# Eight more tiles of the first LayerNorm transposed by DMA, and a new order of all tasks, in a transformer block on one core

## The chip, the cores and the metric

One core of a Trainium2 chip runs the whole kernel. The metric is the device time of one execution in microseconds (us). Five engines work side by side, each through its own list of instructions in order: TensorE (PE; PEld is its loading of weights), VectorE (DVE), ScalarE (ACT), GpSimd (POOL) and SyncE (SP), which here only issues DMAs. The kernel before took 204.36 us, the median of 3 runs (204.16 to 204.45).

## What is computed

The block is an adaptive LayerNorm around linear attention, and a second one around a gated feed-forward layer, for 2048 tokens (S) of 512 channels (D), with 32 heads of 16 and F = 1376:

```python
mod = (silu(c) @ w_mod).reshape(6, 512)          # sa, ca, ga, sb, cb, gb
h = layernorm(x) * (1 + ca) + sa
q, k, v = split(h @ wqkv)                        # 32 heads of 16
pq, pk = q @ w_phi, k @ w_phi                    # per head
phi = lambda p: concat(softmax(p), softmax(-p))
kv, z = sum_s phi(pk) v, sum_s phi(pk)           # over all 2048 tokens
o = (phi(pq) @ kv) / (phi(pq) @ z + 1e-6)
x = x + ga * (o @ wo)
h = layernorm(x) * (1 + cb) + sb
x = x + gb * ((sigmoid(h @ w_gate) * (h @ w_up)) @ w_down)
```

## The kernel before

Tokens are cut into 16 tiles of 128. The kernel is written as a graph of about 1200 small tasks (`G.add`: a name, the engines that can run it, a function, what it reads and writes). The string `ORDER` (lines 40 to 101) lists every task once; `Graph.arrange` goes through it, takes for each task the engine behind an `@` or the first one of its choices, and gives buffers out; `emit` issues the instructions in that order. Each engine then runs its own tasks in the order of the list and waits where an input or a buffer isn't ready. So one string sets the order on all engines, and SP's too.

The stages, by the names of their tasks:

- Loads (`ld_...`, all on SP): x in seven pieces (`x0a` to `x3a`), wk, wv, parts of w_mod (`wm00a` to `wm01b` for sa and ca, `wmga` for ga, `wmm2` for the rest), wo, and the feed-forward weights. All of SP's DMAs go through one queue (q1 of the page).
- `warm`: matmuls on zeros at the start; their results aren't used.
- `modc1.0`, `modc1.1` (line 630): the two halves of sa and ca on TensorE, from the w_mod loads.
- `fold` (line 679): w_phi is multiplied into wq and wk, so that one matmul gives pq or pk. A fold needs the transposed weights `wT_sb`. For the keys (side 1) TensorE transposes them (`tpw`), for the queries (side 0) a DMA does, straight from wqkv in DRAM (`wqT0` to `wqT3`, line 669). `foldc` copies the result on ACT.
- First LayerNorm, for groups of one or two tiles (`LG`): `st1` and `rs1` (statistics), `nmr1`, `xn1` (normalized tile), then the transposition into `h1T`, and `hm1` (times 1+ca plus sa, four tasks a group). The list `TD` says how a group is transposed: 0 by TensorE (`tph`, line 744, into PSUM, from which `hm1` reads on ACT or DVE), 1 by a DMA transpose from SP (`xT1`, line 736, straight into `h1T`, and `hm1` works in place on ACT, POOL or DVE). Before, only groups 6 and 7 (tiles 10 to 13) have a 1.
- Keys and values: for each tile `K` (line 817), `e` (two exponentials on ACT), `n` (sums, DVE line 780), `r` (reciprocal), `phi` (product, POOL or DVE), `V` (line 821), `va`, and `kv` (line 282), which adds into two PSUM banks over all tiles. K of tiles 0 to 7 and V of tiles 0 to 3 are two halves (`K0a`, `K0b`), each with two of the four blocks of channels.
- `kvn`, `kvz`: the sums are masked and go to SBUF. Nothing of the attention's output can start before.
- Queries: `Q` (line 871), `qe`, `qn`, `qphi`, and `pT`, a DMA transpose. Some of them run among the keys, the others later.
- Output, by tile: `num` (line 326), `rd`, `u`, the transposition `oT` (by TensorE for tiles 0 and 1 as `tpo`, else by DMA), `out` (line 356, with wo times ga, made by `wo0` to `wo3` on POOL), `x1_` (residual), `st2`, `rs2`, `nmr2`, `xn2`, `xnT`, `mod` (second LayerNorm).
- Feed-forward, in six chunks of 1, 1, 2, 4, 4 and 4 tiles: `g` and `u` (line 447), `tg` (tanh on ACT, after the table load `tsw`), `hm` (DVE), `y` (line 485), `fin`, `st` (store).

The `warm` tasks, `K`, `V`, `Q` and the folds all stand in TensorE's one list.

Of the kernel before, what the change touches and what calls it, by code (L numbers as in the profile page):

```python
# [43 lines left out]
wqT1 hm1_22 hm1_13@A hm1_03 xn1_7 K1a K0a hm1_02@A hm1_23@A xn1_6 tph42 tph40 xn1_5 hm1_40@A st1_8 tph41 ld_x3a xn1_4 K3a hm1_42 hm1_12@A ld_wv0 nmr1_6 tph43
K3b hm1_41@A xn1_11 tph30 xn1_10 st1_9 rs1_5@P hm1_30@A tph31 wqT3 tph32 K1b ld_wmga st1_15 st1_14 hm1_31@A fold01 foldc01 K0b tph33 wqT2 rs1_8@P K2a K2b
hm1_33 nmr1_5 V0a wqT0 V0b V3a xn1_9 e3.0 V1a xT1_11 e0.0 fold03 n3.0 V1b nmr1_8 xn1_14 va0 e2.0 n0.0 st1_13 r0.0 modca.0 modca.1 xn1_15 st1_12 xn1_8 foldc03
n2.0 modcac e1.0 hm1_32@A V2a fold02 phi0.0 n1.0 r1.0 fold00 V2b foldc02 foldc00 r3.0 va1 xT1_10 hm1_60@P ld_wmm2 va2 r2.0@A hm1_62@P tph82 hm1_82@A tph50
# [1011 lines left out]
```

## Time and profile before

| | |
|---|---|
| median of 3 runs | 204.36 us |
| profiled execution, span from first to last instruction | 202.6 us |
| TensorE busy | 195.7 us, 97% |
| DVE, ACT, POOL busy | 160.4, 106.1, 102.8 us |
| first key matmul | 13.84 us after the span's start |
| last group of `kv` matmuls starts | 56.10 us |
| first gate matmul (`g`) | 67.96 us |
| last `fin` starts | 199.23 us |
| granted TensorE clock | 1.000 |

The profile is of one execution. Its span is measured from the first to the last instruction; the runs' time holds some 1.8 us more. TensorE is called busy while a matmul is in its pipeline, so its share of 97% doesn't say how fast it goes; the distance between starts does. A row of the timeline gives start, length, engine, line, output and inputs, and the number of instructions merged, and in brackets how long the engine was idle before and what ended that.

### The profile page before, as it was taken

How to read it: one execution, taken by the hardware profiler on the slowest of the kernel's cores; microseconds unless marked ns; L12 is line 12 of the kernel's file. 1: busy time of each engine (PE TensorE's matmuls, PEld its weight loads, DVE VectorE, ACT ScalarE, POOL GpSimd, SP SyncE). 2: the span in 40 equal slices, each digit the busy share in tenths (PEclk: the TensorE clock that was granted, in tenths of full speed). 3: DMA queues.
4: the chain of work that ended last, by engine and by line, in shares of the span. 5: the costliest groups of instructions: out<-in, count | busy, mean ns of one | idle time of the engine just before them, and what ended most of it. 6: DMA issues, size and time to landing. Idle time of an engine off the chain costs nothing.

```text
span 202.6 us, 4159 instructions
## 1 busy us (share of the span) xinstructions
PE 195.7 (97%) x1471; PEld 106.2 (52%) x1471; DVE 160.4 (79%) x375; ACT 106.1 (52%) x252; POOL 102.8 (51%) x144
## 2 busy tenths in 40 slices
...
GB/s 173 329 248 265 264 237 119 111 80 290 402 204 71 137 102 59 80 28 108 128 75 84 53 71 84 102 107 53 26 26 81 2 78 52 31 3 22 33 53 55
DMA packets 49452, 22.92 MB, mean 113 GB/s; under 512 B 38065, under 2 KB 47634, under 8 KB 49426
## 3 DMA queue, kind: packets, MB, share of 16 engines
...
## 4 chain that ended last, share of the span: by engine, by line
PE 69%; DVE 14%; ACT 6%; issue 3%; POOL 3%; DMA 3%; SPq 1%; DVEq 0%; POOLq 0%
PE y_ps L485 19%; PE u_ps L447 18%; PE g_ps L447 17%; DVE ks L780 7%; PE a_ps L356 6%; DMA wqk_sb<-in_A_wqkv_dram 3%; PE num L326 2%; DVE kr L798 2%; ACT qe L776 2%; DVE phi L787 2%; PE q_ps L871 1%; PE g_ps L449 1%; ACT h1T L751 1%; DVE qks L780 1%; POOL phi L787 1%
## 5 line engine op out<-in xcount | busy, mean ns | idle before, releaser
L457 ACT ACTIVATE tg<-g_ps 128x512 bf16<-128x512 f32 (+5 forms) x66 | 28.8, 455 | 67.0 <-PE g_ps L447 39.4
L485 PE MATMUL y_ps<-wd_sb,wmod_sb 128*128 128x512 bf16 (+4 forms) x187 | 45.7, 367 | 0.0
L468 DVE SCALAR_TENSOR_TENSOR wmod_sb<-tg,u_ps 128x512 bf16<-128x512 bf16 (+4 forms) x63 | 30.2, 491 | 18.1 <-ACT tg L457 11.6
L447 PEld LDWEIGHTS <-wg_sb 128*128 128x128 bf16 (+1 forms) x252 | 21.9, 99 | 16.1
L447 PEld LDWEIGHTS <-wu_sb 128*128 128x128 bf16 (+1 forms) x252 | 21.9, 99 | 16.0 <-issue 0.3
L784 POOL TENSOR_TENSOR qphi<-qe,qks 128x512 bf16<-128x512 bf16 x24 | 25.1, 1062 | 4.4 <-DMA pT<-qphi 1.7
L485 PEld LDWEIGHTS <-wmod_sb 128*128 128x128 bf16 (+1 forms) x187 | 17.1, 98 | 16.0 <-issue 0.6
L447 PE MATMUL u_ps<-wT_sb,wu_sb 128*128 128x512 bf16 (+2 forms) x124 | 23.8, 322 | 0.0
L447 PE MATMUL g_ps<-wT_sb,wg_sb 128*128 128x512 bf16 (+2 forms) x124 | 23.2, 322 | 0.0
L447 PE MATMUL g_ps<-wqk_sb,wg_sb 128*128 128x128 bf16 (+4 forms) x128 | 20.0, 287 | 0.0
L447 PE MATMUL u_ps<-wqk_sb,wu_sb 128*128 128x128 bf16 (+4 forms) x128 | 19.8, 287 | 0.1
L780 DVE TENSOR_REDUCE qks<-qe 128x64 bf16<-128x1024 bf16 x16 | 19.2, 1206 | 0.0
L492 DVE TENSOR_TENSOR ot<-y_ps,x 128x512 bf16<-128x512 f32 (+2 forms) x17 | 11.1, 654 | 10.2 <-PE y_ps L485 10.1
L780 DVE TENSOR_REDUCE ks<-e 128x64 f32<-128x1024 bf16 (+2 forms) x22 | 19.1, 903 | 0.0
L376 POOL TENSOR_SCALAR ve<-mv 128x2 f32<-128x2 f32 (+1 forms) x8 | 1.8, 221 | 33.8 <-DVE mv L366 33.7
L776 ACT ACTIVATE e<-k_ps 128x512 bf16<-128x512 f32 (+2 forms) x44 | 18.2, 522 | 0.0
L776 ACT ACTIVATE qe<-q_ps 128x512 bf16<-128x512 f32 x32 | 17.4, 618 | 0.6 <-POOL phi L787 0.4
L817 PE MATMUL k_ps<-wqk_f,h1T 128*128 128x512 bf16 x64 | 16.5, 379 | 0.0
L356 PE MATMUL a_ps<-wo_sb,oT 128*128 128x512 bf16 x64 | 16.3, 379 | 0.0
L787 POOL TENSOR_TENSOR phi<-e,kr 128x1024 bf16<-128x1024 bf16 (+2 forms) x10 | 14.4, 1449 | 3.5 <-ACT kr L795 2.0
L821 PE MATMUL v_ps<-wv_sb,h1T 128*128 128x512 bf16 x64 | 16.1, 379 | 0.1
L871 PE MATMUL q_ps<-wqk_f,h1T 128*128 128x512 bf16 x64 | 15.9, 379 | 0.0
...
## 6 DMA issues: line engine op xcount, KB each, us to landing
...
```

The source lines that it names most:

```text
L356: pe.matmul(ap_[:], lhsT=oT[:, j, :], rhs=wo_sb[:, j, :], start=(j == 0), stop=(j == KT - 1))
L447: pe.matmul(ps[:fsz, 0:n], lhsT=w[:, j, ft * P:ft * P + fsz], rhs=h[:, j, 0:n], start=(j == 0), stop=(j == KT - 1))
L457: G.add(f"tg{k}.{ft}", {"ACT": 0.13 + n * 0.00083}, lambda e, tg=tg, g_ps=g_ps, fsz=fsz, n=n: act.activation(tg[:fsz, 0:n], g_ps[:fsz, 0:n ...
L468: dve.scalar_tensor_tensor(hm_all[:fsz, hm[k].slot, ft, 0:n], tg[:fsz, 0:n], 1.0, u_ps[:fsz, 0:n], op0=ALU.add, op1=ALU.mult)
L485: mm = pe.matmul(y[:, 0:c1 - c0], lhsT=hm_all[:fsz, hm[k].slot, ft, tl * P:(tl + 1) * P], rhs=wd_sb[:fsz, ft, c0:c1], start=(ft == 0), sto ...
L776: act.activation(ee[:, a:b, s].rearrange("p g f h -> p g (f h)"), kp[:, a * 64:b * 64].rearrange("p (g n) -> p g n", n=64), ACT.Exp, scale ...
L780: dve.tensor_reduce(ks[:, a:b].rearrange("p g s h -> p (g s) h"), ee[:, a:b].rearrange("p g s f h -> p (g s) h f"), axis=AX.X, op=ALU.add)
L784: engine(e).tensor_tensor(ph[:].rearrange("p (g s f h) -> p g s f h", s=2, f=DH, h=4)[:, :, s], ee[:, :, s], ks[:, :, 1 - s].unsqueeze(2). ...
L787: engine(e).tensor_tensor(ph[:, a * P:b * P].rearrange("p (g f h) -> p g f h", f=DH, h=4), ee[:, a:b].rearrange("p g s f h -> p (g s) f h" ...
L817: pe.matmul(kp[:], lhsT=h1T[:, j, t * P:(t + 1) * P], rhs=wqk_f[:, j, D:2 * D], start=(j == 0), stop=(j == KT - 1))
L821: pe.matmul(vp[:], lhsT=h1T[:, j, t * P:(t + 1) * P], rhs=wv_sb[:, j, :], start=(j == 0), stop=(j == KT - 1))
L871: pe.matmul(qp[:], lhsT=h1T[:, j, t * P:(t + 1) * P], rhs=wqk_f[:, j, 0:D], start=(j == 0), stop=(j == KT - 1))
```

## The change

Two things are changed. In `TD` groups 3, 4, 5 and 8, tiles 4 to 9, 14 and 15, get a 1: their 16 `tph` tasks, of two transposes each, are gone, and eight `xT1` tasks come in. `hm1` of these groups then reads and writes `h1T` in SBUF, so that POOL can run it too. And `ORDER` is another list, found by a search over the order and the engines of all tasks with a replay of measured times. The functions are the same; all lines below the list move up by one.

```diff
-TD = [0, 0, 0, 0, 0, 0, 1, 1, 0]
+TD = [0, 0, 0, 1, 1, 1, 1, 1, 1]
...
-wdz pmem warm0 ld_x0a st1_1 rs1_1 st1_0 c1 c2 ld_x0b warm1_0 warm1_1 warm1_2 warm1_3 ld_wk0 ld_wk1 nmr1_1 xn1_1@A st1_3 warm1_4 st1_2 rs1_0 xn1_0 tph11 tpw1
...
+wdz pmem bd warm0 ld_x0a st1_1 ld_x0b st1_2 rs1_1 st1_3 nmr1_1 st1_0 rs1_2 nmr1_2 c1 c2 xn1_1 warm1_0 warm1_1 warm1_2 warm1_3 ld_wk0 tpw1 c3 ld_x1b st1_7 xn1_2
...
```

Of the 36 `hm1` tasks, before 21 ran on ACT, 8 on DVE and 7 on POOL; now 14, 3 and 19. Of `rs1` three go from POOL to ACT.

First place: SP's list at the start, before. `x_sb` are the loads of x, `wqk_sb` those of wk and of w_mod's ga part, `wmod_sb` those of w_mod, `wT_sb` the transposes of wq, `h1T` those of the first LayerNorm.

```order
L537 DMA x_sb<-in_A_x_dram 128x2x512 x2
L545 DMA wqk_sb<-in_A_wqkv_dram 128x2x512 x2
L537 DMA x_sb<-in_A_x_dram 128x2x512 x2
L542 DMA wmod_sb<-in_w_mod_dram 128x4x256 x2
L537 DMA x_sb<-in_A_x_dram 128x2x512
L542 DMA wmod_sb<-in_w_mod_dram 128x4x256 x2
L537 DMA x_sb<-in_A_x_dram 128x2x512
L669 DMA_TRANSPOSE wT_sb<-in_A_wqkv_dram 128x4x128
L537 DMA x_sb<-in_A_x_dram 128x4x512
L551 DMA wv_sb<-in_A_wqkv_dram 128x4x512
L669 DMA_TRANSPOSE wT_sb<-in_A_wqkv_dram 128x4x128
L555 DMA wqk_sb<-in_w_mod_dram 128x4x512
```

Two more transposes of wq follow there, then those of tiles 11 and 10. The same place now, from w_mod's first loads:

```order
L541 DMA wmod_sb<-in_w_mod_dram 128x4x256 x2
L536 DMA x_sb<-in_A_x_dram 128x2x512 x2
L541 DMA wmod_sb<-in_w_mod_dram 128x4x256 x2
L536 DMA x_sb<-in_A_x_dram 128x4x512
L668 DMA_TRANSPOSE wT_sb<-in_A_wqkv_dram 128x4x128 x2
L550 DMA wv_sb<-in_A_wqkv_dram 128x4x512
L668 DMA_TRANSPOSE wT_sb<-in_A_wqkv_dram 128x4x128 x2
L735 DMA_TRANSPOSE h1T<-xn 128x4x128 x5
L554 DMA wqk_sb<-in_w_mod_dram 128x4x512
L735 DMA_TRANSPOSE h1T<-xn 128x4x128 x2
```

Two loads of x stand ahead of the second pair of w_mod loads, where one stood; the transposes of wq come in the order of blocks 0, 2, then wv, then 3 and 1 (before 1, wv, 3, 2, 0); five transposes of tiles follow before the load for ga.

Second place: TensorE's list among the first keys, before, with buffer numbers, the first matmul of each task. `k_ps` is the output of a K (361, 364, 388 and 443 are tiles 1, 0, 3 and 2), `fold_ps` of a fold (429 is block 1, 472 block 3, 529 and 540 blocks 2 and 0), `v_ps` of a V.

```order
L817 MATMUL k_ps_361<-wqk_f_67,h1T_73 128x512
...
L679 MATMUL fold_ps_429<-bd_101,wT_sb_99 128x128
...
L817 MATMUL k_ps_364<-wqk_f_67,h1T_73 128x512
...
L817 MATMUL k_ps_443<-wqk_f_67,h1T_73 128x512
...
L821 MATMUL v_ps_465<-wv_sb_66,h1T_73 128x512
...
L679 MATMUL fold_ps_472<-bd_101,wT_sb_99 128x128
...
L821 MATMUL v_ps_526<-wv_sb_66,h1T_73 128x512
...
L679 MATMUL fold_ps_529<-bd_101,wT_sb_99 128x128
...
L679 MATMUL fold_ps_540<-bd_101,wT_sb_99 128x128
```

The same place now. `k_ps_358` is tile 1 (its second half), 379 tile 2 and 416 tile 0; `fold_ps_400` and 405 are blocks 0 and 2, 419 and 426 blocks 3 and 1; ahead of these rows stand K1a, K3a, K2a and one pair of transposes.

```order
L816 MATMUL k_ps_358<-wqk_f_67,h1T_73 128x512
...
L678 MATMUL fold_ps_400<-bd_101,wT_sb_99 128x128
...
L678 MATMUL fold_ps_405<-bd_101,wT_sb_99 128x128
...
L816 MATMUL k_ps_379<-wqk_f_67,h1T_73 128x512
...
L816 MATMUL k_ps_416<-wqk_f_67,h1T_73 128x512
...
L678 MATMUL fold_ps_419<-bd_101,wT_sb_99 128x128
...
L678 MATMUL fold_ps_426<-bd_101,wT_sb_99 128x128
...
L816 MATMUL k_ps_416<-wqk_f_67,h1T_73 128x512
...
L820 MATMUL v_ps_442<-wv_sb_66,h1T_73 128x512
```

All four folds of the query side now stand ahead of K0's second half and of every V.

Third place: TensorE's list where the feed-forward begins, before, the first matmul of each task. `tp_x` is xnT0, `a_ps` the output of an `out` (1346 is out2), `q_ps` of a Q, `g_ps` and `u_ps` of `g` and `u`.

```order
L415 MATMUL tp_x_1340<-ident_75,xn2_1330 128x128
...
L356 MATMUL a_ps_1346<-wo_sb_68,oT_1323 128x512
...
L871 MATMUL q_ps_1368<-wqk_f_67,h1T_73 128x512
...
L447 MATMUL g_ps_1373<-wqk_sb_98,wg_sb_69 128x128
...
L447 MATMUL g_ps_1382<-wqk_sb_98,wg_sb_69 128x128
```

And now (`a_ps_1361` is out2):

```order
L414 MATMUL tp_x_1297<-ident_75,xn2_1260 128x128
...
L870 MATMUL q_ps_1309<-wqk_f_67,h1T_73 128x512
...
L870 MATMUL q_ps_1315<-wqk_f_67,h1T_73 128x512
...
L325 MATMUL num_1327<-kvb_74,pT3_1193 128x68
...
L446 MATMUL g_ps_1339<-wqk_sb_98,wg_sb_69 128x128
...
L446 MATMUL g_ps_1344<-wqk_sb_98,wg_sb_69 128x128
...
L446 MATMUL u_ps_1349<-wqk_sb_98,wu_sb_70 128x128
...
L355 MATMUL a_ps_1361<-wo_sb_68,oT_1359 128x512
```

out2 stands behind the first three tasks of the feed-forward, where it stood ahead of them.

More of the change, by code (lines that the diff above doesn't have):

```diff
@@ L44 @@
[L44 to L47, printed above, removed]
@@ L56 @@
-kv14.0 kv15.0 qn6.0 kvn0 kvz0 kv13.4 kv14.4 kv15.4 kvz1 kvn1 num0a num1a num2a wo2 rd0a wo_all rd1a qe3.0 u0a num0b num4a num1b rd0b Q11 qe5.0 rd2a u0b u2a
-rd4a num2b qn3.0 u1a rd1b tpo0 Q8 qphi6.0@P qphi6.1@P oT0 out0 num4b rd2b u1b wd0 qe11.0 u2b qphi3.1@P qphi3.0@P x1_0 rd4b st2_0 qe8.0 Q7 qe7.0 tpo1 oT1 Q10
-Q9 out1 Q15 oT2 rs2_0 qn5.0 nmr2_0 xn2_0 u4a u4b x1_1 qn7.0 tsw xnT0 out2 qphi5.1@P qphi5.0@P pT6 mod02 mod00 qphi7.0@P pT3 mod03@A mod01@A qe15.0 qphi7.1@P
-Q13 g0.8 x1_2 tg0.8 g0.1 st2_1 wd1 rs2_1 tg0.1 u0.8 u0.1 g0.0 num3b g0.4 hm0.1 hm0.8 pT5 qe9.0 tg0.4 g0.9 wd2 u0.4 u0.9 rd3b u3b tg0.9 g0.5 num3a hm0.4 hm0.9
@@ new lines @@
+tpw0 wTc1 warm1_4 wTc0 st1_6 tph13 fold11 foldc11 ld_wk1 tpw3 wTc3 tpw2 fold10 warm1_5 tph10 wTc2 ld_x1a tph11 xn1_3 tph20 st1_4 rs1_4 rs1_0@P nmr1_4 xn1_6
+xn1_7 foldc10 xn1_0 fold12 foldc12 fold13 foldc13 ld_wm00a ld_wm00b modc1.0 modc1c0 tph21 st1_5 tph01 tph03 rs1_3 hm1_10@A tph00 hm1_00@A warm1_6 warm1_7
+hm1_21@A warm1_8 warm1_9 ld_x2a st1_8 tph12 st1_9 rs1_5@P tph02 nmr1_3 xn1_5 tph22 hm1_11@A hm1_01@A xn1_4 ld_x2b st1_10 ld_wm01b ld_wm01a modc1.1 st1_11 K1a
+hm1_20@A K3a modc1c1 hm1_12@A nmr1_5 xn1_9 xn1_8 hm1_13 hm1_22 hm1_02@A rs1_6 K2a tph23 K1b hm1_23@A ld_x3a wqT0 st1_13 e1.0 nmr1_6 xn1_10 wqT2 fold00 fold02
@@ new lines @@
+hm1_03@A foldc00 ld_wv0 wqT3 K2b K0a fold03 foldc03 wqT1 fold01 st1_15 st1_12 foldc01 foldc02 K0b e0.0 V1a V1b va1 xn1_11 rs1_7@P e2.0 V0a V0b n1.0 r1.0 xT1_6
+Q0 V2a xT1_7 hm1_42@P qe0.0 V2b Q2 Q1 st1_14 xT1_5 xT1_4 hm1_31@P n0.0 phi1.0@D nmr1_7 r0.0@A hm1_33@P hm1_41@P hm1_32@P hm1_40@D hm1_43@P V3a xn1_13 n2.0 qn0.0
+phi0.0 hm1_30@P rs1_8 xn1_12 V3b K6a xT1_10 va2 qphi0.0 nmr1_8 xn1_14 ld_wmga modca.0 modca.1 K3b qe2.0 va0 K7a qphi0.1 qn2.0 qphi2.0@P xT1_9 va3 kv0.0 kv1.0
+r2.0@A xT1_8 hm1_53 hm1_50@P modcac xn1_15 qphi2.1 ld_wmm2 hm1_52@P qe1.0 xT1_11 phi2.0@D e3.0 pT0 Q4 V4 V6 va4 qn1.0 qphi1.0@P hm1_61@P qe4.0 n3.0 K7b qn4.0
```

75 lines of the change are left out of this document (37 added, 38 removed).

## The prediction

> **What bounds the kernel now.** I read the page first, then the busy time by windows, TensorE's timeline with its waits, the groups by line, and last the DMA issues with their landings.
>
> The page's first lines, and five rows of the busy time by windows (the columns are sum, then PE, PEld, DVE, ACT and POOL, each with its count, then clock, DMA and GB/s):
>
> ```profile
> span 202.6 us, 4159 instructions
> PE 195.7 (97%) x1471; PEld 106.2 (52%) x1471; DVE 160.4 (79%) x375; ACT 106.1 (52%) x252; POOL 102.8 (51%) x144
> ```
>
> ```profile
> 10.00:20.00 10.00, 9.30 (x95) 5.31 (x94) 9.61 (x32) 9.70 (x26) 9.22 (x17) 1.00 1.33 263
> 20.00:30.00 10.00, 9.81 (x136) 6.32 (x135) 9.90 (x19) 9.91 (x24) 9.24 (x12) 1.00 0.91 254
> 30.00:40.00 10.00, 9.95 (x66) 4.99 (x65) 9.96 (x16) 9.90 (x26) 8.08 (x10) 1.00 0.56 107
> 40.00:50.00 10.00, 10.00 (x82) 5.25 (x81) 10.00 (x19) 9.66 (x34) 8.99 (x7) 1.00 0.79 174
> ...
> 160.00:180.00 20.00, 20.00 (x101) 9.06 (x101) 8.33 (x25) 3.97 (x7) 4.22 (x7) 1.00 0.15 41
> ```
>
> A busy TensorE need not be at its peak, so I take its pace from the starts of its groups. TensorE's timeline at five places:
>
> ```profile
> 13.22 0.55 PE L630 MATMUL modc_ps<-sc_bf,wmod_sb 128*128 128x1 bf16 x16 [0.48 <-ACT h1T L751]
> ...
> 13.84 1.02 PE L817 MATMUL k_ps<-wqk_f,h1T 128*128 128x512 bf16 x4
> 14.70 0.50 PE L744 MATMUL tp_h<-ident,xn 128*128 128x128 bf16 x6
> 15.03 0.59 PE L817 MATMUL k_ps<-wqk_f,h1T 128*128 128x512 bf16 x2
> ...
> 22.30 0.59 PE L821 MATMUL v_ps<-wv_sb,h1T 128*128 128x512 bf16 x2
> 22.91 0.27 PE L744 MATMUL tp_h<-ident,xn 128*128 128x128 bf16 x2
> 23.36 0.27 PE L744 MATMUL tp_h<-ident,xn 128*128 128x128 bf16 x2 [0.18 <-ACT h1T L751]
> ...
> 34.99 2.32 PE L817 MATMUL k_ps<-wqk_f,h1T 128*128 128x512 bf16 x10
> 37.15 0.39 PE L744 MATMUL tp_h<-ident,xn 128*128 128x128 bf16 x4
> ...
> 56.10 1.18 PE L282 MATMUL kvacc<-vaug,phi 128*128 128x68 bf16 x32
> 57.64 0.93 PE L326 MATMUL num<-kvb,pT 128*128 128x68 bf16 x24 [0.36 <-DVE kvb L299]
> ...
> 66.23 1.03 PE L356 MATMUL a_ps<-wo_sb,oT 128*128 128x512 bf16 x4
> 67.10 1.03 PE L871 MATMUL q_ps<-wqk_f,h1T 128*128 128x512 bf16 x4
> 67.96 0.61 PE L447 MATMUL g_ps<-wqk_sb,wg_sb 128*128 128x128 bf16 x8
> ```
>
> Ten matmuls of 512 columns go in 2.16 us (34.99 to 37.15), 0.216 each, and six transposes in 0.33 us (14.70 to 15.03), 0.055 each. At that pace TensorE's row has no hole worth a name from the first key matmul at 13.84 to the sums over the keys at 57.1, except around the transposes at 22.73 to 23.5 (0.5 us). So TensorE sets the pace of the key stage together with DVE and ACT, whose windows are as full; POOL alone has room there, 4.5 us in the 40 us from 10 to 50. After the first gate matmul (67.96) TensorE is the bound alone: from 160 to 180 it is full and the next engine, DVE, is at 8.33 of 20. So whatever work TensorE loses, it gains as time only if nothing else holds it up in the key stage, and whatever wait it gets is paid in full.
>
> **The change part by part.** The profiled execution's span is 202.6; the median of the runs is 204.36. The 1.8 us between them lie outside the span, and I leave them as they are. All terms are put on TensorE's row.
>
> A. Removed: four transposes for each of eight tiles, 32 of 0.055 us, -1.8. All stood behind the first key matmul, in the full part. The new transposes cost TensorE nothing. They sit in SP's queue, whose gap hides them:
>
> ```profile
> 21.30 0.50 SPq L557 DMA_DIRECT2D wo_sb<-in_A_wo_dram  x1
> 29.74 2.51 SPq L736 DMA_TRANSPOSE h1T<-xn  x2
> ```
>
> Eight more at 1.25 us (2.51 for two) are 10 us on a queue that stood idle for 8 us (21.8 to 29.74); pT0 to pT4 come behind them about as early as before. If SP were late by 1 us, the last tiles' h1T would be, which POOL reads next; that is the second rival below.
>
> [...]
>
> B. Moved: the second x2 load (256 KB) now stands in front of the last two loads of w_mod, and the first key matmul stands behind modc1.1, which needs them. TensorE's weight loads show that this wait is on the DMA already, and the page's row of throughput (40 slices of 5.06 us) gives the price:
>
> ```profile
> 13.22 0.47 PEld L630 LDWEIGHTS <-wmod_sb 128*128 128x128 bf16 x16 [0.65 <-DMA wmod_sb<-in_w_mod_dram]
> GB/s 173 329 248 265 264 237 119 111 80 290 402 204 71 137 102 59 80 28 108 128 75 84 53 71 84 102 107 53 26 26 81 2 78 52 31 3 22 33 53 55
> ```
>
> 262 KB at 248 to 329 GB/s are 0.8 to 1.06 us: +0.9. Nothing covers it: the transposes that could stand here stand ahead of it already. So the keys begin at 14.7.
>
> C. Moved: the folds of the query side. They multiply transposed wq, which comes by DMA. Before, fold 1 stood late among the K's and folds 3, 2, 0 among the V's. Now all four stand between K1b and K0b, and the transposes of wq blocks 3 and 1 are the last two of SP's loads. The issues, and the landings of all four, of the second, and of an activation's transpose on a quiet queue:
>
> ```profile
> 8.40 0.84 SPq L537 DMA_DIRECT2D x_sb<-in_A_x_dram  x1
> 9.28 1.51 SPq L669 DMA_TRANSPOSE wT_sb<-in_A_wqkv_dram  x1
> 10.84 0.57 SPq L537 DMA_DIRECT2D x_sb<-in_A_x_dram  x1
> 11.46 0.50 SPq L551 DMA_DIRECT2D wv_sb<-in_A_wqkv_dram  x1
> 12.01 1.62 SPq L669 DMA_TRANSPOSE wT_sb<-in_A_wqkv_dram  x1
> ```
>
> ```profile
> DMA to landing us min/median/max: 5.1/6.3/7.4
> ```
>
> ```profile
> L669 SPq DMA_TRANSPOSE wT_sb<-in_A_wqkv_dram x1: 1621/1621/1621, 12.0 to 12.0; - x1
> ...
> DMA to landing us min/median/max: 7.4/7.4/7.4
> ```
>
> ```profile
> L736 SPq DMA_TRANSPOSE h1T<-xn x1: 1191/1191/1191, 29.7 to 29.7; - x1
> ...
> DMA to landing us min/median/max: 2.4/2.4/2.4
> ```
>
> SP's w_mod loads end where the first x row of this fence begins, 8.4, and with one more x load ahead at 9.3. Then come x3 0.6, two transposes 3.1, wv 0.5: block 3 is issued at 13.7 and block 1 at 15.4, gaps included. TensorE gets to fold 3 at 14.7 plus six half K's (2.6), one pair of transposes (0.1) and two folds (0.4), at 17.8, and to fold 1 at 18.0. When block 1 lands decides: on a quiet queue 2.4 after its issue, 17.8; at the median of these loads 6.3, 21.7. The three behind the first had 1 MB in front of them, wv and wmga; wmga (512 KB, 1.9 us at 265 GB/s) is now issued later, so I take 6.3 - 1.9 = 4.4: 19.8. C = +1.8, with 0 and +3.7 as its ends. Queued behind fold 1 on TensorE are K0b, the V's of tiles 1 and 0 and Q0; ACT's foldc copies and e0 and with them DVE's n0 wait for that too, so no other engine runs ahead.
>
> [...]
>
> D. Gone with A: the hole at 22.73 to 23.5, where transposes waited for ACT: -0.5. What else could wait there, modca's w_mod load, is issued 10 us later but also read 6 us later; I leave that at 0.
>
> E. The hm1 scalings (multiply by 1+ca, add sa), from three groups:
>
> ```profile
> L751 ACT ACTIVATE h1T<-tp_h,modc 128x256 bf16<-128x256 bf16 (+1 forms) x20 | 9.6, 559 | 0.0
> L753 POOL TENSOR_SCALAR h1T<-h1T,modc 128x256 bf16<-128x256 bf16 x7 | 3.8, 556 | 0.0
> L753 DVE TENSOR_SCALAR h1T<-tp_h,modc 128x256 bf16<-128x256 bf16 (+1 forms) x8 | 2.9, 369 | 0.0
> ```
>
> By the list of tasks ACT has 14 in place of 21, DVE 3 in place of 8, POOL 19 in place of 7: ACT -3.9 us, DVE -1.8, POOL +6.7. That lets DVE and ACT follow TensorE if A comes through, and uses POOL's room up (rival 2). On TensorE's row 0.
>
> F. In the change of stages out2 (four matmuls, 0.86) stood ahead of the first gate matmul and now stands behind three; num3b (0.13) went the other way. The first gate matmul doesn't come sooner for that: it waits for the second LayerNorm's chain of out0, x1_0, st2_0, xn2_0, xnT0 and its mods on ACT, in which qe15 and a third mod now stand ahead, while the table load moves behind. So 0.7 us more work is left when the gates begin: +0.7 (0 if the chain gets shorter by that). Two warm-up matmuls went from the first 12 us, where they filled waits, to the gap at 57.1 to 57.6; 0.
>
> The rest, 68 to 199, is the same work in a new order on a TensorE without holes: 0, to either side 0.5.
>
> Sum: -1.8 + 0.9 + 1.8 - 0.5 + 0.7 = +1.1, so the span goes to 203.7 and the time to 205.5.
>
> **The rivals.** 1, faster: the transposes of wq land as on the quiet queue and C is 0. Then the keys end 1.4 us earlier; ACT and DVE can follow, having less to do. For it: it is all that the removed work promises, and 2.4 us was measured. Against: it was measured without loads in front. -1.4 + 0.7, and 0.3 off the gap at 57.1, is -1.0: 203.4. It decides from a landing of block 1 before 18.7, where C is under 0.7 and the sum is 0.
>
> 2, slower by more: POOL becomes the bound of the keys. Its 6.7 us of new hm1's stand against 4.5 us of room, less three rs1's that went to ACT; the last phi on POOL is followed by four products with wo that out0 needs. The rows now:
>
> ```profile
> 55.61 1.16 POOL L787 TENSOR_TENSOR phi<-e,kr 128x512 bf16<-128x512 bf16 x1 [1.27 <-ACT kr L795]
> 56.73 3.40 POOL L851 TENSOR_TENSOR wo_sb<-wo_sb,ga_sb 128x512 bf16<-128x512 bf16 x3
> ```
>
> Now the products end at 60.1 (three of 1.13 after the last phi); with four behind it they would end 1.1 later if the phi's ended when they do now. Each us that POOL idles for an h1T early on adds one: with 1 us of that out0's weights are ready 2.1 us later than now, while A to D have the stage 0.4 later. Of the 1.7 between, 0 to 1.7 shows, since out0 stands in TensorE's row with nothing to fill the wait; I take 1.2: 206.7. It decides once the last phi on POOL ends after 57.5.
>
> 3, no change: C at 0.9 and F at 0.5, so that what A gives is just spent: 204.4.
>
> That the change doesn't do what it says I leave out: the 32 transposes are gone from TensorE's row in the order.
>
> **How the numbers follow.** Forecast 0.41 at 205.5; rival 1 0.28 at 203.4; rival 2 0.14 at 206.7; rival 3 0.17 at 204.4. The runs differ by 0.3 us, so 0.2% (0.4 us) is about what can be told from no change: faster 0.28, same 0.17, slower 0.55. The range reaches from a little under rival 1 to over rival 2, 203.0 to 207.0; past that lie C at its upper end together with POOL's wait above, and no wait at all below.
>
> **What would show it.** Right: modc1.1 near 14.1; TensorE idle for 1 to 3 us ahead of the fold's matmuls between 17.5 and 21, with a DMA of wT_sb as what ended it; the last kvacc matmul between 57 and 58.5; out2 behind the first g_ps. Wrong: the kvacc sums ended by 56, with no wait at the folds (rival 1), or a wait of a_ps for POOL's wo_sb (rival 2), or holes in TensorE's row behind 70.

## The result, and the profile after

| | before | after |
|---|---|---|
| median | 204.26 us (4 runs, 203.75 to 204.45) | 214.47 us (4 runs, 214.25 to 215.35) |
| profiled span | 202.6 us | 212.3 us |
| first key matmul starts | 13.84 | 14.57 |
| last `kv` matmul starts | 57.08 | 63.71 |
| first gate matmul starts | 67.96 | 75.50 |

The change made the kernel slower, by a ratio of 1.0515 (95% interval 1.0482 to 1.0549). The prediction had said slower, but by 1.1 us, with a range up to 207.0; the loss is 10.2 us. (The row of before that starts at 56.10 merges 32 `kv` matmuls, of which the last starts at 57.08.)

The page after, its first lines and the row of the granted clock (40 slices of 5.3 us, in tenths of full speed):

```profile
span 212.3 us, 4121 instructions
PE 200.9 (95%) x1439; PEld 106.8 (50%) x1439; DVE 165.8 (78%) x369; ACT 108.0 (51%) x261; POOL 104.8 (49%) x143
...
PEclk9979999889996999999999999999999999999999
```

This row was full throughout before; now the clock falls three times.

Busy time by windows, after (sum, then PE, PEld, DVE, ACT, POOL, clock, DMA share, GB/s):

```profile
10.00:20.00 10.00, 8.47 (x78) 4.64 (x75) 9.30 (x29) 8.48 (x25) 8.03 (x12) 0.83 1.29 245
20.00:30.00 10.00, 9.60 (x72) 4.57 (x70) 9.03 (x16) 8.94 (x24) 7.46 (x10) 1.00 0.80 174
30.00:40.00 10.00, 9.31 (x99) 5.08 (x97) 9.69 (x12) 8.38 (x19) 9.29 (x11) 1.00 1.12 220
40.00:50.00 10.00, 9.52 (x65) 4.47 (x64) 8.84 (x14) 9.14 (x33) 9.17 (x12) 0.83 0.64 150
...
160.00:180.00 20.00, 20.00 (x100) 8.89 (x99) 12.46 (x33) 5.97 (x10) 3.12 (x6) 1.00 0.12 29
```

TensorE's timeline after, at the places that the prediction spoke of and where it now waits:

```profile
14.11 0.61 PE L629 MATMUL modc_ps<-sc_bf,wmod_sb 128*128 128x1 bf16 x16
14.57 2.52 PE L816 MATMUL k_ps<-wqk_f,h1T 128*128 128x512 bf16 x6
...
19.25 0.83 PE L678 MATMUL fold_ps<-bd,wT_sb 128*128 128x128 bf16 x8 [0.30 <-DMA wT_sb<-in_A_wqkv_dram]
...
39.73 0.82 PE L816 MATMUL k_ps<-wqk_f,h1T 128*128 128x512 bf16 x3 [0.60 <-ACT h1T L750]
41.04 1.89 PE L816 MATMUL k_ps<-wqk_f,h1T 128*128 128x512 bf16 x4 [0.48 <-POOL h1T L752]
...
63.61 0.30 PE L281 MATMUL kvacc<-vaug,phi 128*128 128x68 bf16 x4 [1.79 <-DVE phi L786]
...
76.70 0.38 PE L446 MATMUL u_ps<-wqk_sb,wu_sb 128*128 128x128 bf16 x4 [0.33 <-DVE x L360]
```

No single wait explains 10 us. The stages do better: the start, the keys (from the first key matmul to the last `kv`), the gap to the first gate matmul, and the rest. The same columns, first before, then after:

```profile
0.00:13.84 13.84, 11.12 (x103) 5.61 (x104) 9.69 (x32) 9.70 (x23) 8.98 (x31) 1.00 0.98 243
13.84:57.08 43.24, 42.99 (x398) 23.76 (x396) 42.78 (x87) 42.26 (x115) 36.65 (x41) 1.00 0.89 230
57.08:67.96 10.88, 10.52 (x91) 5.62 (x88) 10.74 (x31) 9.26 (x19) 10.72 (x11) 1.00 0.43 104
67.96:202.56 134.60, 131.09 (x890) 71.25 (x888) 97.21 (x228) 44.87 (x98) 46.48 (x64) 1.00 0.33 63
```

```profile
0.00:14.57 14.57, 11.50 (x98) 6.39 (x99) 10.82 (x35) 9.79 (x26) 9.75 (x31) 0.96 0.97 264
14.57:63.71 49.14, 45.12 (x371) 22.72 (x369) 45.91 (x77) 42.56 (x116) 44.38 (x51) 0.94 0.87 202
63.71:75.50 11.79, 11.79 (x91) 6.29 (x91) 9.60 (x24) 7.52 (x17) 9.15 (x10) 0.86 0.53 145
75.50:212.30 136.80, 132.49 (x894) 71.41 (x890) 99.47 (x235) 48.08 (x103) 41.52 (x55) 1.00 0.30 62
```

Start +0.73, keys +5.90, gap +0.91, rest +2.20: 9.7, the difference of the spans. In the keys DVE has ten instructions fewer (77 for 87) and yet is busy 3.1 us longer; POOL, 6.6 us under the stage's length before (36.65 of 43.24), is busy 7.7 us longer.

DVE's groups of one shape in the key stage, before (phi and qphi are the products of two tensors in SBUF), with count, busy time, mean ns:

```profile
L787 DVE TENSOR_TENSOR phi<-e,kr 128x1024 bf16<-128x1024 bf16 x7 | 4.7, 678 | 0.0
...
L784 DVE TENSOR_TENSOR qphi<-qe,qks 128x512 bf16<-128x512 bf16 x3 | 1.2, 422 | 0.0
...
L787 DVE TENSOR_TENSOR phi<-e,kr 128x256 bf16<-128x256 bf16 x3 | 0.8, 300 | 0.0
L787 DVE TENSOR_TENSOR phi<-e,kr 128x512 bf16<-128x512 bf16 x2 | 0.7, 388 | 0.0
```

And after:

```profile
L786 DVE TENSOR_TENSOR phi<-e,kr 128x1024 bf16<-128x1024 bf16 x7 | 5.9, 850 | 0.5 <-POOL h1T L752 0.4
...
L783 DVE TENSOR_TENSOR qphi<-qe,qks 128x512 bf16<-128x512 bf16 x4 | 3.5, 886 | 0.1
...
L786 DVE TENSOR_TENSOR phi<-e,kr 128x512 bf16<-128x512 bf16 x3 | 3.1, 1045 | 0.1
```

The same shapes take 850 ns for 678, 886 for 422 and 1045 for 388: 12.5 us for 14 tasks, where 15 took 7.4. One of them, on DVE's and on POOL's timeline:

```profile
26.98 2.17 DVE L783 TENSOR_TENSOR qphi<-qe,qks 128x512 bf16<-128x512 bf16 x1
```

```profile
26.96 1.91 POOL L786 TENSOR_TENSOR phi<-e,kr 128x1024 bf16<-128x1024 bf16 x1
28.86 0.73 POOL L752 TENSOR_SCALAR h1T<-h1T,modc 128x256 bf16<-128x256 bf16 x1
```

POOL's product starts 0.02 us ahead of DVE's and ends at 28.87; DVE's ends 0.28 us behind that. The row shows 2.17 us busy and no idle time, for a shape that took 0.42 us before: a stall in it doesn't stand there as a wait. That DVE's product stood still here until POOL's was through, 1.89 us later, is the author's reading of these rows.

SP's list shows something else. The 1.5 MB load of w_mod's last part was issued at 20.67 before and is issued at 26.37 now; of the transposes behind it those of tiles land up to 7.5 us after their issue and those of the queries up to 7.0. The rows of before and after, then the landings of all transposes of the kernel after, tiles first:

```profile
20.67 0.58 SPq L556 DMA_DIRECT2D wmod_sb<-in_w_mod_dram  x1
```

```profile
26.37 0.58 SPq L555 DMA_DIRECT2D wmod_sb<-in_w_mod_dram  x1
```

```profile
DMA to landing us min/median/max: 2.4/2.9/7.5
```

```profile
DMA to landing us min/median/max: 3.0/3.2/7.0
```

So after the first reading there were four suspects: the half clock (G), DVE's products standing still beside POOL (P), transposes landing late behind a big load (Q), and the new list itself (O).

### The profile page after: what moved, and what is told of

Its sections match the earlier page's. It is cut to its first block, busy times and chain, and to the rows that moved or that the text cites. A ratio compares the mean times of both kernels' runs of the same rounds, so it can differ in the third digit from the quotient of the medians.

```text
span 212.3 us, 4121 instructions
## 1 busy us (share of the span) xinstructions
PE 200.9 (95%) x1439; PEld 106.8 (50%) x1439; DVE 165.8 (78%) x369; ACT 108.0 (51%) x261; POOL 104.8 (49%) x143
## 4 chain that ended last, share of the span: by engine, by line
PE 64%; DVE 9%; DMA 8%; SPq 6%; POOL 4%; ACT 4%; issue 3%; DVEq 0%; POOLq 0%
PE y_ps L484 18%; PE g_ps L446 16%; PE u_ps L446 15%; PE a_ps L355 6%; DMA pT<-qphi 3%; PE k_ps L816 3%; DMA wT_sb<-in_A_wqkv_dram 3%; SPq L536 2%; DMA wT_sb<-xn 2%; POOL qphi L783 2%; POOL phi L786 2%; SPq L668 2%; DVE phi L786 2%; DVE qks L779 2%; DVE ks L779 1%
## 5 line engine op out<-in xcount | busy, mean ns | idle before, releaser
L456 ACT ACTIVATE tg<-g_ps 128x512 bf16<-128x512 f32 (+4 forms) x66 | 28.5, 454 | 71.2 <-PE g_ps L446 37.4
L484 PE MATMUL y_ps<-wd_sb,wmod_sb 128*128 128x512 bf16 (+4 forms) x187 | 46.2, 367 | 0.0
L446 PE MATMUL g_ps<-wT_sb,wg_sb 128*128 128x512 bf16 (+2 forms) x124 | 24.0, 322 | 0.0
L446 PE MATMUL u_ps<-wqk_sb,wu_sb 128*128 128x256 bf16 (+4 forms) x128 | 20.1, 287 | 0.3 <-DVE x L360 0.3
L816 PE MATMUL k_ps<-wqk_f,h1T 128*128 128x512 bf16 x64 | 18.6, 423 | 1.2 <-ACT h1T L750 0.6
L446 PE MATMUL g_ps<-wqk_sb,wg_sb 128*128 128x128 bf16 (+4 forms) x128 | 19.4, 287 | 0.2
L870 PE MATMUL q_ps<-wqk_f,h1T 128*128 128x512 bf16 x64 | 17.0, 400 | 0.0
L786 POOL TENSOR_TENSOR phi<-e,kr 128x1024 bf16<-128x1024 bf16 (+2 forms) x12 | 15.7, 1328 | 1.2 <-DVE phi L786 0.8
L820 PE MATMUL v_ps<-wv_sb,h1T 128*128 128x512 bf16 x64 | 15.6, 379 | 0.0
L332 DVE TENSOR_TENSOR o<-num,den 128x256 bf16<-128x256 f32 x32 | 13.1, 417 | 0.7
```

The source lines that it names most:

```text
L446: pe.matmul(ps[:fsz, 0:n], lhsT=w[:, j, ft * P:ft * P + fsz], rhs=h[:, j, 0:n], start=(j == 0), stop=(j == KT - 1))
L456: G.add(f"tg{k}.{ft}", {"ACT": 0.13 + n * 0.00083}, lambda e, tg=tg, g_ps=g_ps, fsz=fsz, n=n: act.activation(tg[:fsz, 0:n], g_ps[:fsz, 0:n ...
L484: mm = pe.matmul(y[:, 0:c1 - c0], lhsT=hm_all[:fsz, hm[k].slot, ft, tl * P:(tl + 1) * P], rhs=wd_sb[:fsz, ft, c0:c1], start=(ft == 0), sto ...
L786: engine(e).tensor_tensor(ph[:, a * P:b * P].rearrange("p (g f h) -> p g f h", f=DH, h=4), ee[:, a:b].rearrange("p g s f h -> p (g s) f h" ...
L816: pe.matmul(kp[:], lhsT=h1T[:, j, t * P:(t + 1) * P], rhs=wqk_f[:, j, D:2 * D], start=(j == 0), stop=(j == KT - 1))
L820: pe.matmul(vp[:], lhsT=h1T[:, j, t * P:(t + 1) * P], rhs=wv_sb[:, j, :], start=(j == 0), stop=(j == KT - 1))
```

## The experiments

Times are medians; each stands beside runs of the kernel before on the same chip (204.1 to 204.4), and the ratio is to these. "List" is `ORDER`. The diffs show the main places of an edit. The profile is of one execution of each run.

**More matmuls on zeros, in the list.**

```diff
-... modc2.1 modc2c K9 ...
+... modc2.1 modc2c wx_6 wx_7 wx_8 K9 ...
```

> The kernel after, with 19 more matmuls on zeros (0.216 us each at full clock) where TensorE idled: six between 9.9 and 13.4 us, three ahead of K9 and two ahead of K11 (37.3 to 40.7), eight ahead of the last kv task (61.2 to 63.6). Theory G (the clock is granted in stretches of 3.41 us by how busy TensorE was in the stretch before; the three stretches at half clock after such idle times cost 1.5 us each): no stretch at half clock, mean granted clock above 0.99, time 209.5 to 211. Theory W (the waits alone set the time, and the half clock lies in time that TensorE would have waited anyway): the clock is full, but the time stays at 214 to 214.7, since later waits only grow. If the matmuls delay more than they keep up: above 214.7.

218.04 us, 1.0677 (1.0626 to 1.0728): worse, the last of the three cases. Each added task takes a PSUM bank, and the third ahead of K9 waited 1.84 us for ACT to free one, so the hole grew and two stretches at half clock came with it (40.31 to 47.14). A matmul that needs a bank isn't filler. G wasn't tested by this.

**The big load later.**

```diff
-... qphi2.1 ld_wmm2 hm1_52@P ... xT1_15 hm1_80 modc2.0 modc2.1 modc2c K9 ...
+... qphi2.1 hm1_52@P ... xT1_15 ld_wmm2 hm1_80 K9 ... K10 modc2.0 modc2.1 modc2c ...
```

> The kernel after, with the 1.5 MB load of w_mod's last part moved on SP from ahead of the transposes of tile 11, pT0, pT2, 14 and 15 to behind them, and the 48 one-column matmuls that use it (modc2) from ahead of K9 to behind K10. Theory Q (DMA transposes queued behind that load land 7 us after their issue instead of about 3, so POOL gets its buffers and ACT and POOL their h1T late, and K9, K11 and the end of the keys wait): transposes of tile 11, pT0 and pT2 land in 2 to 4 us, the waits of 0.60 and 0.48 us ahead of K9 and K11 are gone, the last kv matmul comes 1.5 to 3 us earlier than 63.7, time 211 to 212.8. Rival (the end of the keys is set by DVE's and POOL's own work or by the order): landings quick, but the last kv matmul within 0.7 us of 63.7 and time 213.8 to 215.

218.21, 1.0683 (1.0596 to 1.0769). The transposes that had stood behind the load landed in 3.3, 3.1 and 4.0 us, as Q expects, but two others now stood behind it, and POOL waited for the first of these, pT1, which landed at 45.29 (an expectation below calls it the second):

```profile
45.45 3.79 POOL L786 TENSOR_TENSOR phi<-e,kr 128x1024 bf16<-128x1024 bf16 x2 [3.14 <-DMA pT<-qphi]
```

Q's mechanism is seen, its price in the kernel after isn't.

**The end of the keys.**

```diff
-... kv11.0 Q6 e15.4 ... phi15.0@D qe6.0 qn6.0 V12 ... r15.4@A phi15.4@D kv15.4 ...
+... kv11.0 V12 Q6 e15.4 ... phi15.0@D r15.4@A qe6.0 phi15.4@D qn6.0 ... kv15.4 ...
```

> The kernel after, with three places of its list changed at the end of the keys: r15.4 on ACT ahead of the exponentials of query tile 6, phi15.4 on DVE ahead of the sums of query tile 6, and V12 on TensorE ahead of Q6. Theory O (the list puts query work ahead of the last key products, so TensorE waits 1.96 us ahead of the last kv task, and that idle stretch halves the clock for the next 3.41 us): the wait is gone or under 0.4 us, no half clock behind 61 us, time 211.3 to 212.8. Rival (the products are late because POOL and DVE are full, so another of them takes its place): the last kv task still waits 1 us or more on DVE or POOL phi, time 213.8 to 214.7.

214.39, 1.0503 (1.0458 to 1.0548): nothing gained. The 1.79 us wait for phi became one of 2.33 us for ACT's vaug. The rival's time held, though what took the place was neither POOL nor DVE but ACT. This trace has one stretch at half clock where the one after had three, and took 214.04 us against 214.30; that already spoke against G as the main cause.

**The kernel before with eight of its matmuls on zeros gone.**

```diff
-for i in range(12): warm(f"warm1_{i}", ...)
+for i in range(4): warm(f"warm1_{i}", ...)
```

> The kernel before without eight of its twelve single matmuls on zeros (warm1_4 to warm1_11, which all run ahead of 13 us). Theory G: at least one stretch of 3.41 us between 8 and 20 us falls to half clock, granted clock 0.975 to 0.992, and the keys begin or go on later: time 204.5 to 206.5. Rival (such short idle times don't lower the clock; the matmuls only fill idle time): full clock from 5 us on, time 203.9 to 204.4.

206.61, 1.0114 (1.0081 to 1.0146), 0.1 us over G's range, with two stretches at half clock from 11.65 to 18.48, around the start of the keys (13.74). Four matmuls of 512 columns go in 1.71 us there (13.74 to 15.45), 0.43 each where 0.216 was the pace, and the keys grow from 43.2 to 45.6 us. So here, where TensorE has no slack, the half clock did cost. A price for each stretch doesn't follow: two of the four executions had a mean clock of 0.992, which is one stretch (half of 3.41 us in 204.6), and took 206.44 and 206.49; the two with two stretches (0.983) took 206.74 and 206.81.

**hm1 from POOL to ACT.**

```diff
-... hm1_42@P ... hm1_31@P ... hm1_33@P hm1_41@P hm1_32@P ...
+... hm1_42@A ... hm1_31@A ... hm1_33@A hm1_41@A hm1_32@A ...
```

> The kernel after, with the twelve hm1 tasks of groups 3, 4, 5 and 8 that ran on POOL put on ACT; list and transposes unchanged. Theory P (DVE's products phi and qphi, which read two tensors from SBUF, stand still while POOL works, up to 2.17 us for a task of 0.42; POOL's twelve more hm1 tasks make such meetings frequent, and DVE bounds the keys): DVE's phi and qphi tasks between 14 and 64 us take 1.5 to 3.5 us less than the 12.6 us that they take in the kernel after, the last kv matmul comes 1.5 to 4 us earlier than 63.7, time 210.5 to 213. Rival (ACT, with 7 us more work, takes POOL's place, or the late landings decide): last kv matmul within 1 us of 63.7 or later, time 214 to 217.

217.19, 1.0595 (1.0509 to 1.0681): the rival. TensorE now waited for ACT too (h1T 1.07, vaug 1.02 and 0.87 us), and ACT has no room either. DVE's products still took 12.4 us.

**The big load last of all.**

```diff
+... xT1_13 ld_wmm2 ... kv14.4 modc2.0 modc2.1 modc2c wmod_free r15.4@A ...
```

> The kernel after, with the 1.5 MB load of w_mod's last part on SP behind all transposes of the first LayerNorm (behind tile 13) and the 48 one-column matmuls that use it ahead of the last kv task, where TensorE waited 1.96 us. In the run with this load behind tile 15, pT1 and pT4 came to stand behind it, landed 7.1 and 7.6 us after issue, and POOL waited 3.14 us for the second; here no transpose that the keys wait for stands behind it. Theory Q (late landings behind this load cost the kernel after 1 to 2.5 us): pT and h1T transposes land in 2.4 to 4 us, POOL's waits on DMA between 30 and 45 us go, last kv matmul at 61 to 62.7, time 211.5 to 213.5. Rival (they cost nothing there, since DVE bounds the keys): landings quick, last kv matmul 63.2 to 64.5, time 213.8 to 215.

220.65, 1.0758 (1.0671 to 1.0845). Last kv at 65.45, and a pT of the queries now waited in the queue: TensorE stood 3.79 us for it ahead of 80.75. Neither theory had that.

**The new list with TensorE's transposes.**

```diff
-TD = [0, 0, 0, 1, 1, 1, 1, 1, 1]
+TD = [0, 0, 0, 0, 0, 0, 1, 1, 0]
-... xT1_4 ...
+... tph30 hm1_30@A tph31 hm1_31@A tph32 hm1_32@A tph33 hm1_33 ...
```

> The kernel after with TD as in the kernel before: tiles 4 to 9, 14 and 15 transposed by TensorE again, at the place of their DMA transposes in the list, with hm1 on ACT and DVE as before; the rest of the list is that of the kernel after. Theory D (the DMA transposes and what they bring, late h1T and hm1 on POOL, cost most of the 10 us): time 205 to 210, last kv matmul at 56 to 60. Theory O (the new list is at fault, whoever transposes): time 212 to 216, last kv matmul 61 to 65.

227.74, 1.1112 (1.1028 to 1.1196), outside both ranges.

**The old list with the DMA transposes.**

```diff
-TD = [0, 0, 0, 0, 0, 0, 1, 1, 0]
+TD = [0, 0, 0, 1, 1, 1, 1, 1, 1]
-... tph40 ... wqT0 V0b ...
+... wqT0 xT1_6 xT1_7 xT1_5 xT1_4 V0b ...
```

> The kernel before with only TD changed: eight tiles more by DMA in the old list, the transposes of tiles 6, 7, 5, 4 on SP behind those of wq, the others behind their xn1, hm1 of these groups on ACT and DVE as before (groups 4 and 3 moved behind hm1_60). The big load of w_mod comes behind ten transposes on SP instead of two. Theory D: time 206.5 to 212, with TensorE waiting for h1T among the first keys. Theory O (the new list is at fault): time 203 to 205, within 0.7 us of the kernel before.

216.54, 1.0586 (1.0466 to 1.0706): slower than theory D's range. TensorE waited 2.88 us for h1T and 6.70 us for the big load, which SP reached only behind ten transposes. Together the last two say: each half of the change, placed as here, is worse than the whole. They don't put the fault on "the list" or "the transposes" alone, and an edit that moves tasks can't say what the whole paid for. So the next runs leave the list untouched and take away the suspected cost itself, most of them by leaving out work that the block needs.

**Work inside TensorE's waits, list untouched.**

```diff
 def f_k(e, js=range(KT), t=t, kp=kp):
+    for _ in range({9: 3, 11: 2}.get(t, 0)):
+        pe.matmul(kp[:], lhsT=<zeros>, rhs=<zeros>, start=True, stop=True)
```

> The kernel after with its list untouched; inside three tasks TensorE does matmuls on zeros ahead of the instruction that waited: three of 0.216 us in K9, two in K11 (into the bank that the task overwrites), sixteen of 0.1 us ahead of the last kv task (adding zeros to unused columns). Theory G (half clock costs what the trace shows it doing, 1.5 us a stretch, in the two stretches from 40.7 and 64.6 us): those stretches run at full clock, time 211 to 213. Rival (DVE or POOL bounds the keys, so TensorE at half clock only fills time in which it would wait): full clock there, last kv matmul within 0.6 us of 63.7, time 213.0 to 214.6, the gain only behind the last kv.

214.84, 1.0482 (1.0416 to 1.0547). The stretch from 64.6 was at full clock and the gap to the first gate shrank from 11.79 to 10.46 us, but the last kv came at 65.20 (the first key at 15.41), and the stretch from 40.5 stayed at half. No gain, but only one of the two stretches was mended, so this alone doesn't settle G.

**POOL's hm1 shortened.**

```diff
+if e == "POOL":
+    dst, src = dst[:, 0:16], src[:, 0:16]
```

> The kernel after with its list untouched; the 19 hm1 tasks on POOL work on 16 of 256 columns, the rest of these blocks stays as the transpose left it (so the part of the scaling that POOL did is left out). POOL gives back up to 19 x 0.5 us. Theory P (POOL's hm1 tasks delay h1T and hold up DVE's two-input products): DVE's phi and qphi between 14 and 64 us take 2 us less or better, last kv matmul 59 to 61.5, time 208.5 to 212. Rival (late landings and the list's own order decide): last kv matmul 62.5 to 64, time 213 to 214.8.

214.55, 1.0451 (1.0356 to 1.0545): the rival. DVE's products still took 12.2 us. So it isn't the hm1's that hold them up most, but POOL's own products (phi, qphi, wo), which the new list puts beside them; the row at 26.98 above is such a meeting. The trace after says the same: of the 5.0 us that its 14 tasks take over the durations of before, 4.8 fall on tasks that ran mostly beside a product of POOL. In the trace before, none of the 15 tasks is longer than its group's mean by more than 0.04 us. One execution here took 211.77 us, at a clock of 0.992 where the others had 0.976; why stays open.

**A third of the big load.**

```diff
-sp.dma_start(wmod_sb[:, :, 3 * D:], wmod_v[:, :, 3 * D:])
+sp.dma_start(wmod_sb[:, :, 3 * D:4 * D], wmod_v[:, :, 3 * D:4 * D])
```

> The kernel after with its list untouched; the load of w_mod's last part takes 0.5 MB instead of 1.5 MB (modc2 uses that third for all its columns, so the second modulation is another). Theory Q (this load holds up the transposes issued behind it): transposes of tile 11, pT0 and pT2 land 3 to 4 us after issue instead of 7.5, 7.0 and 5.2, POOL's wait of 0.71 us on pT goes, last kv matmul 61 to 63, time 211.5 to 213.7. Rival (nothing that bounds waits for them): landings quick, time 213.9 to 214.8.

214.70, 1.0482 (1.0403 to 1.0561): the rival again. One execution had the full clock (1.000) and took 213.02; the others, at 0.973 to 0.984, 214.67 to 215.54. So with no stretch at half clock 8.8 us are still lost: G as the main cause falls.

**All three.**

> The three edits of the runs before together (matmuls on zeros in K9, K11 and ahead of the last kv; POOL's hm1 on 16 columns; the third of the load). If the three causes add up and are the main ones: last kv matmul 57.5 to 60, time 206 to 209.5. If the new list itself is slow (its keys begin later, its order of query work and its waits behind 75 us stay): 210 to 214.

212.72, 1.0403 (1.0347 to 1.0459), the second range, with the clock full throughout in the trace. Last kv at 62.11. With three suspects treated some 8 us are left.

**DVE's products exchanged.**

```diff
+if e == "DVE":
+    dve.tensor_reduce(<phi as float32>, <e as float32>, axis=AX.X, op=ALU.add)   # one input, same length
```

> The kernel after with its list untouched; the phi and qphi products that run on DVE are left out and a reduction of the same number of elements per ns stands in their place (128x512 or 128x256 elements of 4 bytes, one input, about 0.67 and 0.37 us), which needs no second tensor from SBUF and doesn't wait for the reciprocal. Theory P (DVE's two-input products stand still while POOL reads: 12.6 us for 14 tasks instead of 7.5, and DVE bounds the keys): these tasks take 7 to 8 us, last kv matmul at 58 to 61, time 208.5 to 212. Rival (DVE has slack, something else bounds): the tasks are as short, but the last kv matmul comes at 62.5 to 64.5, time 213 to 215.

210.88, 1.0312 (1.0230 to 1.0393). DVE's groups in this run:

```profile
L786 DVE TENSOR_REDUCE phi<-e 128x512 f32<-128x512 f32 x7 | 4.7, 674 | 1.1 <-DMA pT<-qphi 1.0
...
L786 DVE TENSOR_REDUCE qphi<-qe 128x256 f32<-128x256 f32 x4 | 1.6, 406 | 0.0
...
L786 DVE TENSOR_REDUCE phi<-e 128x256 f32<-128x256 f32 x3 | 1.1, 377 | 0.0
```

7.4 us in place of 12.5, the last kv at 60.06, and 3.6 us of the 10.2 are gone. Without any filler, no stretch behind 16 us is at half clock in this trace, so the later half clocks can come from these stalls; another execution, at 0.976, lost as much clock as three stretches would and took 212.32. P holds, as one cause. The exchange does more than end DVE's stalls, though. POOL is held up in such meetings too: its hm1 of 256 columns in the keys took 632 ns each after and take 565 here, its phi of 512 columns 1303 and 1051, so the gain is that of both engines. And the wait for the reciprocal is gone as well; after, DVE idled only 0.7 us ahead of all these products together, so that can be a small part at most.

**All four.**

> All four edits in the kernel after: matmuls on zeros in TensorE's waits, POOL's hm1 on 16 columns, the third of the w_mod load, and reductions in place of DVE's products. The three edits without the last gave 212.7. If the stalls of DVE are the main cause of what is left: last kv matmul 56.5 to 59.5, time 206 to 209.5. If the list itself is slow: 210 to 213.

210.47, 1.0280 (1.0210 to 1.0350), in the second range. An explanation is that the matmuls on zeros (2.7 us) now find no wait to fill; the run without them below bears it out.

**The control: the same exchange in the kernel before.**

> The same exchange of DVE's products for reductions in the kernel before, as the control. Its 15 tasks take 7.7 us there, next to what they take undisturbed. Theory P: little changes, time 203.3 to 204.4. If leaving out the wait for the reciprocals is what helps: below 203.

204.32, 0.9990 (0.9965 to 1.0016), 10 runs. Nothing: in the old list DVE's products are not held up, and their wait for the reciprocals costs nothing there. So what the exchange gained in the kernel after is a cost that the new list brought.

**One group alone, old list.**

```diff
-TD = [0, 0, 0, 0, 0, 0, 1, 1, 0]
+TD = [0, 0, 0, 0, 0, 0, 1, 1, 1]
-... xn1_14 ... xn1_15 ...
+... xn1_14 xT1_14 ... xn1_15 xT1_15 ...
```

> The kernel before with one part of the change: only group 8 (tiles 14 and 15, needed last) by DMA, each transpose on SP behind its xn1, hm1 on ACT and DVE as before, list otherwise untouched. TensorE loses 8 transposes, 0.44 us. SP's load of w_mod's last part comes behind four transposes instead of two and reaches its place 2.5 us later. If a transpose by DMA that is needed late costs nothing: 203.6 to 204.4. If the transposes hold up SP's loads and what stands behind them: 205 to 209.

210.91, 1.0325 (1.0233 to 1.0417), above the second range: two DMA transposes cost 6.5 us. SP's and TensorE's timelines:

```profile
17.32 7.77 SPq L736 DMA_TRANSPOSE h1T<-xn  x4
25.14 0.57 SPq L556 DMA_DIRECT2D wmod_sb<-in_w_mod_dram  x1
```

```profile
32.12 0.85 PE L616 MATMUL modc_ps<-sc_bf,wmod_sb 128*128 128x1 bf16 x24 [4.16 <-DMA wmod_sb<-in_w_mod_dram]
```

SP waits in its list for the tiles' xn, the load goes out at 25.14 instead of 20.67, TensorE stands 4.16 us, and two stretches at half clock (30.03 to 36.86) follow.

**Three edits without the filler.**

> The kernel after, list untouched, with reductions in place of DVE's products, POOL's hm1 on 16 columns and the third of the w_mod load, without the matmuls on zeros (2.7 us of work that in the run with all four had no wait left to fill). If the stalls beside POOL are the main cause and the rest is the later start of the keys and the waits behind the first gate: last kv matmul 57.5 to 59.5, keys 43 to 44.5 us long, time 207 to 209.5; no stretch at half clock behind 20 us, since the waits that led to them are gone. If the list has another cost of its own among the keys: 209.5 to 211.

207.35, 1.0186 (1.0150 to 1.0221). The stages:

```profile
0.00:14.46 14.46, 11.31 (x98) 6.07 (x99) 10.59 (x35) 9.79 (x26) 9.56 (x31) 0.98 1.01 263
14.46:58.39 43.93, 42.80 (x371) 22.34 (x368) 40.56 (x77) 41.19 (x115) 36.30 (x50) 0.97 0.85 174
58.39:68.86 10.47, 10.43 (x90) 5.50 (x90) 9.44 (x24) 8.88 (x20) 8.77 (x9) 1.00 0.93 284
68.86:205.30 136.44, 132.33 (x893) 71.46 (x891) 98.56 (x235) 48.02 (x103) 42.26 (x56) 1.00 0.30 62
```

The time and the length of the keys lie where they were expected: the keys are down to 43.93 us, 0.7 over before. POOL's shortened hm1 and the smaller load, worth nothing that shows each by itself, are worth 3.5 us once DVE's stalls are gone: against the run with reductions alone 0.8 in the start, 0.8 in the keys and 1.5 behind the first gate, in the two traces. The 0.8 in the start is within what the start of this list varies by itself (first key at 14.12 to 15.41). Against the run with all four edits (210.47) the filler alone cost 3.1 us, so the 8 us that were left with three suspects treated can hold some of that.

**One group alone, its transposes behind the loads.** The diff is against the run with one group above.

```diff
-... xn1_14 xT1_14 ... xn1_15 xT1_15 ... ld_wo ...
+... xn1_14 ... xn1_15 ... ld_wo xT1_14 xT1_15 ... K8 hm1_80@A hm1_82@A ...
```

> As the run with group 8 alone by DMA in the old list (210.9), but with its two transposes behind the loads of w_mod's last part and wo on SP, and hm1_80 and hm1_82 on ACT behind K8. Theory S (SP's list held the 1.5 MB load up by 4.5 us, TensorE waited 4.16 us for it ahead of modc2 and then ran two stretches at half clock): the load is issued at 20.7 us again, that wait is under 0.5 us, no half clock, time 203.6 to 204.6. Rival (a transpose by DMA costs by its own landing or by hm1 in place): 205.5 to 210.

205.40, 1.0061 (1.0045 to 1.0077). The load goes out at 20.77, the clock is full, and 5.5 of the 6.5 us are back: the mechanism of S holds. The time is in neither range, 1.3 us over before; TensorE waits 0.5 us for ACT there and starts its keys 0.3 us later, the rest wasn't followed up. No version tried beats the kernel before.

## Why the prediction was wrong

- **What bounds the kernel** was half right. It named TensorE, DVE and ACT together for the key stage, then kept its whole sum on TensorE's row. On DVE's row the 5.9 us by which the stage grew are 3.1 us more of busy time and 2.8 us more of idle time; with DVE's products exchanged, the stage went from 49.14 to 44.77 us.
- **A** (-1.8) right: 32 matmuls fewer on the page (1439 for 1471). It bought nothing that shows, in a stage where DVE had no room.
- **B** (keys at 14.7, +0.9) right: modc1.1 at 14.11 as forecast, first key at 14.57, +0.73. Other runs with nearly this list spread from 14.12 to 15.41 there, so the size of the hit is in part luck.
- **C** (+1.8) right in the landing, in part by luck, and wrong in the wait. The landing of block 1 was taken at 19.8 (issue at 15.4 and 4.4 us); it was 19.6 (14.6 and 5.0): two errors that nearly cancelled. But TensorE waited 0.30 us in the row at 19.25, and little ahead of it: at half clock from 13.36 to 16.77 it got there late itself. In the run with filler, short hm1 and small load, at full clock, the wait for wT_sb was 1.4 us.
- **D** right: no hole at 22.7.
- **The transposes "in SP's queue, whose gap hides them"** failed. The queue had room, but its order mattered: the 1.5 MB load, issued at 20.67 before, stood behind them and went out at 26.37, right ahead of tile 11, pT0 and pT2, which landed 7.5, 7.0 and 5.2 us after issue. "pT0 to pT4 come behind them about as early as before" was true of the issue and not of the landing. By itself this cost nothing that can be measured (a third of the load: 214.70); with DVE's stalls gone it may be part of the 3.5 us, which weren't split between load and hm1.
- **E** is the step that failed most: "That lets DVE and ACT follow TensorE". It added up the hm1's by engine, each at its old duration, and let DVE have 1.8 us less to do. That part came, but DVE's products took 5.1 us more, because the new list puts POOL's products beside them, so DVE was 3.1 us longer busy in a stage where it had no room, and the last kv came at 63.71, not between 57 and 58.5. POOL's own sum was short as well: its 19 hm1's in the keys took 632 ns each and not 556, 11.8 us where 3.8 stood, so 8.0 more and not 6.7. The hm1's moved to POOL are not what stalled DVE: shortened to a sixteenth, they left its products at 12.2 us for 14 tasks. 3.6 us of the loss go with DVE's products, 7.1 with these and the two edits on POOL and the load together.
- **F** (+0.7) right as far as it goes: out2 stands behind the first gates. But the rest was taken as 0 to either side 0.5, and from the first gate to the end the kernel after needs 2.2 us more, of which F explains 0.7. The gate stage began with new waits, one of 0.33 us in the row at 76.70.
- **Rival 2** had the right place (last phi on POOL behind 57.5: it ended at 59.7) and the wrong mechanism: out0 started at 68.49, 3.9 us after POOL's last product with wo at 64.6, so nobody waited for these. Its price was for one wait at the end of the stage, not for stalls of DVE all through it.
- **The half clock** was in no part of the prediction, since the trace before shows none.

What stays open: the run with three edits still loses 3.1 us. Its trace accounts for 2.7 of them (start 0.6, keys 0.7 and rest 1.8, less 0.4 in the gap), which were not tested one by one. And why the search's replay took this list for a better one can't be seen from runs; durations measured in another order would hold neither the stalls beside POOL nor the late landings, but that is argued and not shown.
